# Seven products instead of eight for two more chunks, one of the sums moved to TensorE, and a new order of all steps

## The chip, the core and the metric

The kernel runs on one core of one Trainium2 chip. The metric is device time in microseconds, the median over runs; lower is better. Five engines work side by side, each in the order of its own queue: TensorE (PE, matrix products from on-chip memory into the PSUM banks), VectorE (DVE), ScalarE (ACT), GpSimd (POOL) and SyncE (SP). In this kernel POOL and SP mostly issue transfers (DMAs). An engine waits on semaphores for what another engine or a transfer has to finish first.

## The reference, cut to what matters

```
phi(x) = where(x > 0, x, exp(x) - 1) + 1          # = min(exp(x), max(x, 0) + 1)
kv  = einsum('bhsd,bhse->bhde', phi(k), v)        # per head: 64 x 64
z   = sum over s of phi(k)
x   = (phi(q) @ kv) / (phi(q) . z + 1e-6)         # 8 sequences, 8 heads, 576 x 64 each
a   = x @ w1 ;  b = x @ w2                        # x is 4608 x 512, w1 and w2 are 512 x 1024
out = ((a * b) @ w3) @ w_out                      # 1024 x 1024, 1024 x 512
```

Linear attention on 8 sequences, then a feed-forward part whose two branches are multiplied element by element. w3 @ w_out does not depend on the tokens.

## The kernel before, in words

The 4608 tokens are worked as nine chunks of 512. Chunks 0 to 7 are the first 512 tokens of sequences 0 to 7; chunk 8 collects the remaining 64 of each. All matrix products take bf16 and sum in f32.

At the start w3 @ w_out is folded once into a 1024 x 512 matrix (wf_sb): steps w transpose a block of w3 on TensorE (L143 to L148), steps u multiply it with w_out (L150 to L157), two matmuls of 512 columns a step.

The attention of a sequence b is made of small steps. L, M, N load k, q, v in halves of 512 KB (L97), R loads the last 64 tokens of the eight heads, 64 KB a transfer (L108). x and X take exp on ScalarE (L175), y and Y the max part on VectorE (L181), z and Z their min (L199), v casts v (L212). K sums phi(k) times v over the tokens (L227). T transposes phi(q) by a DMA (L266); for sequences 0 and 1, a does it on TensorE (L271). A multiplies phi(q) by kv for 128 tokens and divides (L288): four matmuls, then three VectorE instructions (L324 to L326); it uses the two "at" PSUM banks, of which there is one pair. D transposes the result by a DMA (L344), for sequences 0 and 1 step P on TensorE (L337).

A gate unit F c.f (L370) makes 128 of the 1024 gate columns of chunk c: eight matmuls of 512 columns (four for a, four for b), a ScalarE copy of a (L367), and a VectorE multiply of that copy with b in PSUM (L368).

Chunks 6, 7 and 8 make their gates differently. The 2 x 2 block product is done with seven products of half-size blocks instead of eight (the Strassen-Winograd scheme). Steps e form four combinations of the blocks of w1 and of w2 once (L386), steps d four combinations of a chunk's x (L398), each one VectorE instruction. A step G c.q.i (L435) is product i of column block q: four matmuls of 256 columns, a pair for each branch (L410). Products 1, 3, 5 and 7 add up in one PSUM bank ("u", one of the two banks that output units use as well, L444), product 2 has a bank of its own ("t"), products 4 and 6 share a third ("t2"); t and t2 are two of the four "mm" banks. The order of a block is fixed by its sums: the bank u after product 1 is copied out by ScalarE (L450); so it is after product 3, and t2 after product 4. VectorE adds such a copy to the bank after product 2, 5 or 6 (L454). A step m c.q.i (L462) multiplies the two halves of such a sum, out of SBUF, into the gate. After product 7 the bank u is multiplied directly: ScalarE copies its a half (L458), VectorE multiplies it with the b half in PSUM (L459). The f32 copies and sums live in a ring of twelve half tiles that takes six slots of the load pool "ld" (L427).

An output unit O c.m (L532) multiplies 128 tokens' gates with wf_sb: eight matmuls of 512 columns and one copy. S, H store results; Q is the last output unit, in two halves with a store each.

The order is written out by hand: the string ORDER (L577) names every step, and each engine's queue gets its instructions in that order. A "+" behind a step chooses the other engine for its copy (VectorE instead of ScalarE) or the other queue for its load (POOL instead of SP). B, C, E are the loads of w1/w2, w_out and w3, always on POOL; they cast f32 to bf16. I are constants. GATES (L613) lets the load M2.1 wait for the weights' load B0.0.

Of the kernel before, what the change touches and what calls it, by code (L numbers as in the profile page):

```python
# [20 lines left out]
def kernel(  # L21
# [403 lines left out]
    ring = []  # L425

    def fsm(name):  # L427
        if not spare.get("ring"):
            spare["ring"] = True
            for n in range(6):  # L430
                t = from_ld(("f", n), [P, 2, 2, HN], F32)
                ring.extend((t[:, 0], t[:, 1]))
        return ring.pop(0)

    def g_unit(c, q, i):  # L435
# [3 lines left out]
        a, m, name, first = ((), ((0, 0, 0), (0, 0, 0), "u", True), ((0, 0, 1), (0, 1, 0), "t", True),  # L439
# [8 lines left out]
        if i in (1, 3, 4):  # L448
            s = st["s", i] = fsm("gs")
            nc.scalar.copy(out=s, in_=t)  # L450
        elif i in (2, 5, 6):
            s = st["c", i] = fsm("gc")
            o = st["s", {2: 1, 5: 4, 6: 3}[i]]
            nc.vector.tensor_tensor(out=s, in0=o, in1=t, op=ALU.add)  # L454
            ring.append(o)
        else:
            s = fsm("ga")
            nc.scalar.copy(out=s[:, 0], in_=t[:, 0])  # L458
            nc.vector.tensor_mul(out=abs_[c][:, q + 4, 0:HN], in0=s[:, 0], in1=t[:, 1])  # L459
            ring.append(s)  # L460

    def g_mul(c, q, i, alt):  # L462
        s = cs_[c, q]["c", i]
        f, r = {2: (q, 0), 5: (q + 4, 1), 6: (q, 1)}[i]
# [125 lines left out]
    A3.0 O1.2 A3.2 L4.1 v4.2+ F2.6 A3.3 F2.3 N4.1 y4.0 F2.1 M4.0 x4.0 A3.1 x4.1 F2.0 M4.1 y4.2 v5.2+  # L590
    x4.2 F2.7 Y4.0 D3.0 F2.4 z4.0 F2.2 X4.1 Y4.1 S1.0 F2.5 v4.1 Z4.1 N4.0 M5.0 X4.0 Z4.0 A3.4 z4.2
    y4.1 O2.3 F3.7 z4.1 M5.1 v4.0 A2.4 Y5.0 F3.6 L5.0 T4.0 M6.1 R6.0+ x5.2 Y5.1 X5.0 F3.1 N5.1 Z5.0
    S1.1 O2.2+ K4 F3.2 M6.0 x6.2 X5.1 A4.2 Z5.1 F3.4 z5.2 F3.5 y5.0 A4.1 F3.0 L5.1 F3.3 N5.0 y5.1
    X6.1 y6.2 O2.1 A4.3 R6.1+ N6.0 S2.1 x5.1 N6.1 v5.0+ T5.0 O2.0 x5.0 v5.1+ A4.0 R7.0+ z5.1 D4.0
    z5.0 X6.0 O3.3 y7.2 O3.2+ K5+ S2.0 L6.0 z6.2 O3.1 A5.2 L6.1 O3.0 A5.1 D1.1 Y6.1 Z6.1 F4.2 A5.0
    Y6.0 F4.5 y6.1 F4.7 v6.0+ x6.1 L7.0 x6.0 M7.0 A5.3 D3.1 x7.0 z6.1 F4.0 v6.1+ v6.2 F4.6 A4.4 Z6.0
    F4.1 S3.0 F4.4 D5.0 A5.4 y6.0 z6.0 F4.3 M7.1 F5.7 x7.2 y7.0 Y7.0 z7.2 L7.1 N7.0 K6+ z7.0 F5.6
    F5.0 y7.1 X7.1 X7.0 Z7.0 F5.5 S3.1 F5.3 Y7.1 T6.0 R7.1+ Z7.1 A6.3 T7.0 F5.1 O4.2 A6.1 x7.1 O4.1
    A6.2 e1.0 e0.0 v7.0 F5.4 A6.0 z7.1 O4.3 e0.1 F5.2 e1.1 v7.2+ O4.0 N7.1 S4.1 e0.2 e0.3 e1.2 D6.0
    d6.0 v7.1 A6.4 e1.3 O5.1 O5.0 G6.1.1 G6.1.2 d6.1 G6.0.1 K7 d6.2 d6.3 G6.0.2 G6.0.3 m6.1.2 G6.0.4  # L600
    m6.0.2 S5.0 A7.3 G6.1.3 G6.0.5 G6.1.4 G6.1.5 m6.0.5 G6.2.4 G6.0.6 G6.0.7 G6.1.7 A7.0 G6.1.6
    G6.2.1 S4.0 G6.3.1 D5.1 G6.2.2 G6.2.3 G6.3.2 G6.3.3 m6.1.6 G6.2.5 G6.3.4 m6.2.2 G6.3.5 G6.2.6
    G6.2.7 A7.4 D7.1 G6.3.7 G6.3.6 O5.2 m6.3.5 A7.2 d8.0 O5.3 d8.2 G8.0.1 G8.0.4 m6.2.6 d8.1 m6.0.6
    d8.3 A7.1 G8.1.1 m6.3.6 G8.0.3 G8.0.2 G8.1.3 m6.2.5 G8.1.4 G8.0.5 G8.1.5 G8.3.4 G8.1.6 m8.0.2
    G8.0.7 G8.1.7 G8.2.4 m6.1.5 D7.0 G8.1.2 m8.0.5 d7.0 G8.2.1 S5.1 G8.3.1 G8.0.6 G8.2.3 m8.0.6
    G8.2.6 G8.3.3 G8.2.5 m6.3.2 G7.0.4 G8.3.5 G7.1.4 m8.1.2 G8.2.7 d7.1 G8.2.2 G8.3.7 d7.2 m8.1.5
    G8.3.6 O6.0 m8.3.5 m8.1.6 d7.3 O6.3 m8.2.5 O6.2+ m8.3.6 m8.2.6 O6.1 G7.0.1 m8.2.2 G8.3.2 G7.1.1
# [122 lines left out]
```

## Time and profile before

| | |
|---|---|
| median of three runs | 250.67 us (249.24 to 251.13) |
| span of the profiled execution | 248.0 us |
| TensorE busy | 230.9 us, 1548 matmuls |
| VectorE busy | 187.4 us, 434 instructions |
| ScalarE busy | 131.9 us, 213 instructions |
| GpSimd busy | 49.4 us, 79 instructions |
| matmuls of the gate units (L362) | 384 of 512 columns |
| matmuls of the seven-product steps (L422) | 336 of 256 columns |
| matmuls of the output units (L536) | 280 of 512 columns |

The profile is of one execution; its span goes from the first to the last instruction, and no total time is given for that execution. The page first gives busy time by engine, then 40 equal slices of the span with the busy share of each engine in tenths. Groups of instructions have a line, an engine, the tiles written and read, a count, the busy time, the mean length in ns, and the idle time before them with what ended it. "The chain" is the work that ended last, followed back step by step. "The waits" list who waited for whom. Matmuls overlap one another, so the time that TensorE needs for one is read from the spacing of starts and not from its length; the same holds, to a lesser degree, for VectorE.

### The profile page before, as it was taken

To read this page: it belongs to the slowest core of one execution; us is meant where nothing else is said; L and a number is where in the kernel's file an instruction comes from. 1 tells how busy PE (TensorE), PEld (TensorE's weight loads), DVE (VectorE), ACT (ScalarE), POOL (GpSimd) and SP (SyncE) were. 2 spreads that over 40 slices of the span, in tenths; PEclk is the share of its full clock that TensorE was granted. 3 is DMA by queue.
4 is the path that set the end of the run, shared out by engine and by line. 5 is a ranking of instruction groups with operands and counts; after the bars stand their busy time and mean duration, and the time that the engine had idled before them with its cause. 6 is when DMAs were issued, how large, how long until landed. Compare 5 with 4: busy or idle time off the path is not lost.

```text
span 248.0 us, 4281 instructions
## 1 busy us (share of the span) xinstructions
PE 230.9 (93%) x1548; PEld 133.6 (54%) x1548; DVE 187.4 (76%) x434; ACT 131.9 (53%) x213; POOL 49.4 (20%) x79
## 2 busy tenths in 40 slices
PE   0699868999999999999999999999999999999994
PEld 0445455654454554345445544545488688578542
DVE  3227769777898847788768799988899999779810
ACT  2206667658756725675563383536466377245321
POOL 8546368665014050500000000000000000000000
PEclk9999988999999999999999999999999999999999
DMA  7999999999999999999999999917750133040144
GB/s 159 193 202 310 295 211 211 194 259 288 287 219 329 236 234 273 217 304 282 288 362 268 284 270 221 295 37 174 169 193 0 22 65 107 3 169 1 44 152 145
DMA packets 64021, 49.43 MB, mean 199 GB/s; under 512 B 32480, under 2 KB 58848, under 8 KB 64000
## 3 DMA queue, kind: packets, MB, share of 16 engines
q1 hardware_dynamic: 52928, 36.31, 58.3%
q0 software_dynamic: 10928, 12.72, 25.2%
q8 instruction: 12, 0.20, 0.3%
q10 hardware_dynamic: 144, 0.13, 0.2%
q14 instruction: 9, 0.07, 0.1%
HBM read 38.80 MB, written 9.44 MB: 194 GB/s over the span
## 4 chain that ended last, share of the span: by engine, by line
PE 67%; DMA 21%; ACT 3%; DVE 3%; SPq 2%; issue 2%; POOL 0%; ACTq 0%; DVEq 0%; POOLq 0%
PE o_ps L536 21%; PE a_ps L362 12%; PE b_ps L362 12%; DMA q<-in_q_dram 10%; PE gu L422 9%; DMA w3b<-in_moe_w_dram 7%; PE gt L422 6%; DMA k<-in_k_dram 4%; PE nd L310 3%; PE kvp L245 2%; SPq L104 1%; ACT e L179 1%; PE o_ps L561 1%; PE kvp L249 1%; DVE qj L209 1%
## 5 line engine op out<-in xcount | busy, mean ns | idle before, releaser
L536 PE MATMUL o_ps<-wf_sb,ab 128*128 128x512 bf16 x280 | 64.2, 379 | 0.0
L362 PEld LDWEIGHTS <-w_sb 128*128 128x128 bf16 x384 | 36.5, 98 | 40.6 <-issue 0.8
L362 PE MATMUL a_ps<-xt,w_sb 128*128 128x512 bf16 x192 | 50.3, 379 | 0.5 <-ACT a_sb L367 0.5
L362 PE MATMUL b_ps<-xt,w_sb 128*128 128x512 bf16 x192 | 50.3, 379 | 0.0
L536 PEld LDWEIGHTS <-ab 128*128 128x128 bf16 x280 | 26.8, 98 | 29.3
L368 DVE TENSOR_TENSOR ab<-a_sb,b_ps 128x512 bf16<-128x512 f32 x48 | 32.5, 683 | 11.5 <-PE b_ps L362 5.9
L538 ACT COPY o_sb<-o_ps 128x512 f32<-128x512 f32 x30 | 17.4, 585 | 42.8 <-PE o_ps L536 28.8
L367 ACT COPY a_sb<-a_ps 128x512 f32<-128x512 f32 x48 | 27.7, 585 | 22.2 <-PE a_ps L362 21.8
L326 DVE TENSOR_TENSOR xn<-nd,r 128x512 bf16<-128x512 f32 x30 | 20.7, 691 | 1.0
L422 PEld LDWEIGHTS <-spare 128*128 128x128 bf16 x192 | 18.7, 98 | 2.2
L179 ACT ACTIVATE e<-q 128x1024 bf16<-128x1024 f32 x16 | 16.8, 1057 | 5.7 <-DMA q<-in_q_dram 5.0
L310 PE MATMUL nd<-kv,qt 128*128 128x130 bf16 (+1 forms) x160 | 16.6, 228 | 2.9 <-ACT kv L254 1.8
L179 ACT ACTIVATE e<-k 128x1024 bf16<-128x1024 f32 x16 | 16.8, 1056 | 3.2 <-DMA k<-in_k_dram 3.1
L310 PEld LDWEIGHTS <-qt 128*128 128x128 bf16 (+1 forms) x160 | 11.8, 103 | 12.2 <-issue 3.5
L454 DVE TENSOR_TENSOR spare<-spare,gt 128x512 f32<-128x512 f32 x24 | 16.1, 680 | 1.8 <-PE gt L422 0.9
L154 PE MATMUL wf_ps<-wt_sb,w3t 128*128 128x512 bf16 x64 | 16.5, 403 | 0.6 <-DMA wt_sb<-in_moe_w_out_dram 0.6
L450 ACT COPY spare<-gu 128x512 f32<-128x512 f32 x24 | 13.6, 587 | 3.9 <-PE gu L422 3.7
L422 PEld LDWEIGHTS <-w_sb 128*128 128x128 bf16 x144 | 14.0, 98 | 2.7 <-issue 0.3
L465 DVE TENSOR_TENSOR ab<-spare 128x256 bf16<-128x256 f32 x36 | 14.1, 417 | 0.1
L114 POOL DMA_DIRECT2D qk32r<-in_q_dram x14 | 9.0, 644 | 23.3 <-ACT a_sb L367 10.7
L209 DVE TENSOR_TENSOR qj<-e,y 128x512 bf16<-128x512 bf16 x32 | 12.1, 418 | 2.0 <-ACT e L179 1.8
L422 PE MATMUL gu<-spare 128*128 128x256 bf16 x96 | 13.4, 272 | 0.0
(87 smaller groups left out, 294.0 us busy)
## 6 DMA issues: line engine op xcount, KB each, us to landing
out_dram<-o_sb SPq DMA_DIRECT2D x15, 512.0 KB, 3.9
q<-in_q_dram SPq DMA_DIRECT2D x13, 512.0 KB, 8.1
k<-in_k_dram SPq DMA_DIRECT2D x12, 512.0 KB, 7.0
v<-in_v_dram SPq DMA_DIRECT2D x12, 512.0 KB, 9.0
w3b<-in_moe_w_dram POOLq DMA_DIRECT2D x8, 256.0 KB, 10.0
k<-in_k_dram POOLq DMA_DIRECT2D x4, 512.0 KB, 9.1
w_sb<-in_moe_w_dram POOLq DMA_DIRECT2D x8, 256.0 KB, 7.5
q<-in_q_dram POOLq DMA_DIRECT2D x3, 512.0 KB, 12.6
```

The lines of the kernel that those rows point to most:

```text
L154: nc.tensor.matmul(wfs[i], w3ts[i][:, kc, :], wo_sb[:, kc, :], start=(kc == 0), stop=(kc == FC - 1))
L179: nc.scalar.activation(out=e, in_=x, func=AF.Exp)
L209: nc.vector.tensor_tensor(out=p[0][:, 2 * g + c].rearrange("p j u d -> p u j d"), in0=e[:, c], in1=y[:, c], op=ALU.min)
L310: nc.tensor.matmul(nds[g][rows, i * 2 * E1:(i + 1) * 2 * E1], w, kvs[b % 2][:, i, g].rearrange("p u e -> p (u e)"), start=True, stop=True)
L326: nc.vector.tensor_tensor(out=dst.rearrange("p (g h) e -> p g h e", g=2), in0=v4[:, :, :, 0:D], in1=r[rows].unsqueeze(3).to_broadcast([n, ...
L362: nc.tensor.matmul(ps, w[:, kc, f * P:(f + 1) * P], xt_of(c)[:, :, kc, :], start=(kc == 0), stop=(kc == KC - 1))
L367: nc.scalar.copy(out=a_sb, in_=a_ps)
L368: nc.vector.tensor_mul(out=abs_[c][:, f, :], in0=a_sb, in1=b_ps)
L422: nc.tensor.matmul(t[:, w], l, r, start=(first and w == 0 and k == 0), stop=(k == 1), skip_group_check=True)
L454: nc.vector.tensor_tensor(out=s, in0=o, in1=t, op=ALU.add)
L536: nc.tensor.matmul(o_ps, ab[:, f, m * P:(m + 1) * P], wf_sb[:, f, :], start=(f == 0), stop=(f == FC - 1))
L538: copy_of(alt)(out=rows_of(c, m // 2)[:, m % 2], in_=o_ps)
```

## The change

Three things are done together.

1. Chunks 4 and 5 also make their gates with the seven products: F4.* and F5.* go, d4.*, d5.*, G4.*, G5.*, m4.*, m5.* come. Chunks 0 to 3 keep the gate units.
2. In all five such chunks, product 2 no longer has a VectorE add. After product 1 ScalarE copies bank u into an "mm" bank instead of into SBUF, and the four matmuls of product 2 accumulate onto that bank. Its result is then treated like that of product 7: ScalarE copies the a half, VectorE multiplies it with the b half in PSUM; these copies use the small tiles of the gate units ("f", four of them). The steps m c.q.2 vanish. The ring has eight half tiles, in four slots of the load pool. The combinations of w1 are kept in the tile that held w_out, so that only those of w2 take slots of the load pool.
3. ORDER is new from the first step to the last. It begins with loads of k and q beside those of w3 and w_out, so that the attention of sequence 0 (K0) comes ahead of the products u. The loads L2 to L5, L6.1, M2 to M6, N2 to N5 and N6.0 (28 loads) go from SP to POOL, as do R0.0 and R0.1; R6.1, R7.0 and R7.1 go from POOL to SP. Some copies change engine (K0 to VectorE; K1, K5, K6 to ScalarE; some of O, P, a, u, v, w). The order of the chunks (0 to 6, then 8, then 7) stays.

```diff
@@ ws_make
+        if w == 0:
+            s[i] = wt_sb[:, i].rearrange("p a n -> p (a n)").rearrange("p (k n) -> p k n", k=2)
+        else:
+            s[i] = from_ld(("w", w, i // 2), [P, 2, 2, NQ * P], BF16)[:, i % 2]
@@ fsm
-            for n in range(6):
+            for n in range(NR):                       # NR = 4
@@ g_unit
-        ... ((0, 0, 1), (0, 1, 0), "t", True),
+        ... ((0, 0, 1), (0, 1, 0), "t", False),
-        if i in (1, 3, 4):
+        if i == 1:
+            st["t"] = mm_ps.tile([P, 2, HN], F32, tag="mm", name="gt")
+            nc.scalar.copy(out=st["t"], in_=t)
+        elif i in (3, 4):
             s = st["s", i] = fsm("gs")
             nc.scalar.copy(out=s, in_=t)
-        elif i in (2, 5, 6):
+        elif i in (5, 6):
             s = st["c", i] = fsm("gc")
-            o = st["s", {2: 1, 5: 4, 6: 3}[i]]
+            o = st["s", {5: 4, 6: 3}[i]]
             nc.vector.tensor_tensor(out=s, in0=o, in1=t, op=ALU.add)
             ring.append(o)
         else:
-            s = fsm("ga")
-            nc.scalar.copy(out=s[:, 0], in_=t[:, 0])
-            nc.vector.tensor_mul(out=abs_[c][:, q + 4, 0:HN], in0=s[:, 0], in1=t[:, 1])
-            ring.append(s)
+            s = sm.tile([P, NCH], F32, tag="f", name="a_sb", bufs=4)[:, 0:HN]
+            nc.scalar.copy(out=s, in_=t[:, 0])
+            nc.vector.tensor_mul(out=abs_[c][:, q if i == 2 else q + 4, 0:HN], in0=s, in1=t[:, 1])
```

The new order, its start and the stretch in which chunks 4 and 5 are gated:

```
E3 L0.0+ x0.0 R0.0+ C1 L0.1+ R0.1+ y0.1 I0 y0.0 E0 M0.1+ E5 N0.0+ N0.1 C0 z0.0 E7 x0.1 C3 z0.1
C2 E1 M0.0 Y0.0 I1+ M1.1+ E6 Y0.1 X0.0 E2 M1.0+ Z0.0 R1.1+ X0.1 L1.0+ x0.2 v0.2 L1.1+ Z0.1 B3.1
y0.2 z0.2 w0+ B3.0 R1.0+ N1.1 N1.0 w3 w5+ K0+ a0.0+ B2.0 B2.1 E4 a0.1 u5.0 u5.1 u0.0 w7+ a0.2
...
O3.3 O3.2 S3.1 v5.1+ x6.2 N5.0+ z5.0 v5.0 O2.3 Y5.0 M6.0+ Z5.0 z5.2 T5.0 x6.1 z5.1 A4.4 N7.1
d4.0 z6.2 X6.0 L6.0 O3.0 d4.1 O3.1 G4.0.1 K5 G4.1.1 S3.0 d4.2 Y6.1 Z6.1 Y6.0 Z6.0 G4.0.3 y6.1
d4.3 G4.0.4 N6.1 A5.3 G4.0.2 G4.1.3 G4.0.5 G4.1.4 A5.2 G4.1.5 G4.0.7 G4.0.6 D3.1 N6.0+ G4.1.2
A5.1 G4.3.4 G4.1.7 v7.1 O2.2 y6.0 A5.0 m4.0.6 z6.1 G4.3.1 G4.1.6 R6.1 G4.2.1 G4.3.3 m4.0.5
G4.3.2 G4.2.3 G4.3.5 m4.1.6 D5.0 N7.0 G4.2.4 G4.2.5 G4.2.2 G4.3.7 v6.2 G4.3.6 G4.2.7 v6.1 d5.0
d5.1 m4.2.5 x6.0 G4.2.6 O4.1 z6.0 m4.1.5 G5.0.1 G5.0.4 G5.1.1 G5.0.3 m4.3.6 d5.2 T6.0 v6.0+ d5.3
...
G5.3.4 A6.2 m5.0.6 G5.3.5 G5.3.2 Y7.0 v7.0 L7.1 O4.0 M7.1 y7.2 G5.3.6 G5.3.7 x7.2 m5.3.6 A5.4
z7.2 R7.1 D6.0 m5.2.6 d6.0 X7.1 S4.0 O5.0 m5.1.6 x7.1 O4.3 d6.1 v7.2 d6.3 O4.2 d6.2 Y7.1 Z7.1
...
K7 G6.2.3 m5.1.5 m5.3.5 m5.2.5 D5.1 O5.3 G6.2.5 G6.2.2 G6.3.1 G6.2.6 G6.2.7 A7.4 G6.3.3 D7.1
...
m8.2.5 O8.1 S8.0 O8.2+ H8.2 O8.3 H8.3 O7.2+ H7.2 Q7.3
```

More of the change, by code (lines that the diff above doesn't have):

```diff
@@ L425 @@
     ring = []
+    NR = 4
     def fsm(name):
@@ L438, in g_unit @@
         st = cs_.setdefault((c, q), {})
-        a, m, name, first = ((), ((0, 0, 0), (0, 0, 0), "u", True), ((0, 0, 1), (0, 1, 0), "t", True),
+        a, m, name, first = ((), ((0, 0, 0), (0, 0, 0), "u", True), ((0, 0, 1), (0, 1, 0), "t", False),
                              ((1, 1), (1, 1), "u", False), ((1, 0), (1, 0), "t2", True),
@@ L604 @@
[L604 to L607, printed above, removed]
-    m8.3.2 G7.0.3 S6.0 G7.0.6 G7.1.3 G7.0.5 G7.0.2 G7.1.5 G7.3.4 m7.1.5 G7.0.7 G7.2.4 m7.0.6 G7.1.7
-    G7.1.6 m7.0.2 G7.2.1 G7.2.2 G7.3.1 S6.1 m7.2.2 G7.2.3 G7.2.6 G7.3.3 G7.2.5 G7.3.6 G7.3.5 G7.2.7
```

57 lines of the change are left out of this document (27 added, 30 removed).

## The prediction

> **What bounds the kernel now.** I read the page's engine totals and slices first, then the busy time by stretch, the waits, and last the chain in order of time.
>
> ```profile
> span 248.0 us, 4281 instructions
> PE 230.9 (93%) x1548; PEld 133.6 (54%) x1548; DVE 187.4 (76%) x434; ACT 131.9 (53%) x213; POOL 49.4 (20%) x79
> PE   0699868999999999999999999999999999999994
> DVE  3227769777898847788768799988899999779810
> PEclk9999988999999999999999999999999999999999
> ```
>
> The reader is to see a TensorE row that is full from the seventh slice to the last but one, and a VectorE row that reaches 9 only after the twenty-third. A busy PE need not be a PE at its rate, so the next view is the chain, where the pieces are spaced by what the array really took:
>
> ```profile
> 61.23 0.86 PE a_ps L362 x4
> 62.09 0.86 PE b_ps L362 x4
> 184.68 0.87 PE gu L422 x8
> 185.55 0.44 PE gt L422 x4
> 230.68 12.09 PE o_ps L536 x56
> ```
>
> Here 56 matmuls of 512 columns take 12.09 us, 0.216 each, and a matmul of 256 columns takes 0.87/8 = 0.109. The gate units (L362) run at the same 0.86/4 = 0.215. So in these stretches TensorE runs without holes, and work taken from it is worth its full length, as long as nothing else becomes late. What else could be late is seen by stretch (columns: stretch, length, then busy time and instructions of PE, PEld, DVE, ACT, POOL):
>
> ```profile
> 98.00:131.00 33.00, 31.80 (x175) 15.14 (x174) 26.16 (x57) 20.80 (x32) 3.94 (x6) 1.00 1.10 295
> 131.00:180.00 49.00, 49.00 (x284) 24.29 (x282) 43.30 (x99) 23.66 (x37) 0.00 (x0) 1.00 0.90 211
> 180.00:212.00 32.00, 32.00 (x289) 26.48 (x287) 30.67 (x72) 19.86 (x39) 0.00 (x0) 1.00 0.26 75
> ```
>
> From 180 to 212 us, where chunks 6 and 8 are gated by seven products, VectorE is busy 30.67 of 32 us (96%), and TensorE still does not stop: both engines are at their limit there. From 131 to 180, with chunks 4 and 5 gated plainly, VectorE has 5.7 us free. That is the room the change spends. What TensorE waited for after the start is little:
>
> ```profile
> PE nd L310 <- DVE xn L326: 0.8, 2, 0.5
> PE a_ps L362 <- ACT a_sb L367: 0.5, 1, 0.5
> PE nd L310 <- DVE xnr L326: 0.2, 1, 0.2
> ```
>
> These add to 1.5 us.
>
> **The change part by part.**
>
> *TensorE, chunks 4 and 5.* Removed: 16 gate units (F4.*, F5.*) of 8 matmuls, 128 x 0.216 = 27.6 us. Added: 56 products (G4.*, G5.*) of 4 matmuls of 256 columns, 224 x 0.109 = 24.4 us. Net -3.2 us. Every other TensorE step is there as often as before; products of chunks 6 to 8 are the same.
>
> *VectorE.* Durations overlap with the next instruction's, so I take the spacing of starts where the engine has no idle time (rows of the timeline; the two without an operation name are pieces of the chain):
>
> ```profile
> 195.85 0.42 DVE L459 TENSOR_TENSOR ab<-spare,gu 128x256 bf16<-128x256 f32 x1
> 196.19 0.68 DVE L454 TENSOR_TENSOR spare<-spare,gt 128x512 f32<-128x512 f32 x1
> 196.78 0.42 DVE L465 TENSOR_TENSOR ab<-spare 128x256 bf16<-128x256 f32 x1
> 197.12 0.16 DVE L324 TENSOR_SCALAR r<-nd 128x8 f32<-128x8 f32 x1
> 197.31 0.20 DVE L325 RECIPROCAL r<-r 128x8 f32<-128x8 f32 x1
> 197.55 0.69 DVE L326 TENSOR_TENSOR xn<-nd,r 128x512 bf16<-128x512 f32 x1
> 34.44 0.76 DVE qj L209 x2
> 35.20 0.60 DVE y L184
> 46.30 1.28 DVE L368 TENSOR_TENSOR ab<-a_sb,b_ps 128x512 bf16<-128x512 f32 x2 [0.63 <-ACT a_sb L367]
> ```
>
> An add of 512 columns costs 0.59, a multiply of 256 columns 0.34, an attention block (A) 0.19 + 0.24 + 0.6 = 1.04, a max step (y) 0.60, a min step (z, a pair whose second half overlaps) 0.67, a plain gate multiply 1.28 - 0.68 = 0.60. A difference of x (d) I put at 0.34, the multiply's price, since it covers 512 bf16 columns as one L209 does (0.76/2 at most).
> Chunks 4 and 5: minus 16 x 0.60; plus, for both, 8 differences, 16 adds (products 5, 6) and 32 multiplies (products 2, 5, 6, 7): 16 x 0.59 + 40 x 0.34 = 23.0. Net +13.4. Chunks 6 to 8: product 2 loses its add, and its multiply stays, 12 x 0.59 = -7.1. Together +6.3 us: VectorE goes from 187.4 to about 194 of 248.
>
> *ScalarE.* Chunks 4, 5: minus 16 copies of 512 columns, plus 24 (products 1, 3, 4), plus 16 of 256 (products 2, 7); chunks 6 to 8: plus 12 of 256.
>
> ```profile
> L450 ACT COPY spare<-gu 128x512 f32<-128x512 f32 x24 | 13.6, 587 | 3.9 <-PE gu L422 3.7
> L458 ACT COPY spare<-gu 128x256 f32<-128x256 f32 x12 | 4.5, 373 | 4.9 <-PE gu L422 4.2 <-DVE ab L459 0.5
> ```
>
> That is 8 x 0.587 + 28 x 0.373 = +15.1, to 147 of 248: hidden behind TensorE while ScalarE has two fifths of its time free. No row shows a ScalarE copy that writes PSUM. The bounds are the 256-column copy (0.37) and twice the 512-column one (1.17); I take 0.587, the same size from the same bank. At the upper end the 20 such copies add 12 us to an engine that still has 89 free. New is that product 2 waits for this copy. In the new order the closest pair (G4.3.1, G4.3.2) has three products between, 1.3 us of TensorE against 0.59 of copying; it is hidden unless ScalarE is 0.7 us behind. What stands behind a late product 2 is every matmul, since TensorE's queue is in order.
>
> *The stretch where both engines are full.* In the new order I sum the steps from O2.3 up to O5.3 (the rest of chunk 2's output, chunks 4 and 5 gated, the attention of sequences 5 to 7, the first half of chunk 6). Two more prices from the chain:
>
> ```profile
> 109.92 0.41 PE nd L310 x4
> 133.84 0.45 PE kvp L245 x8
> 134.29 0.11 PE kvp L249
> 134.40 0.45 PE kvp L245 x8
> ```
>
> TensorE: 10 output units, 73 products, 11 attention blocks, 3 kv sums, 10 x 1.73 + 73 x 0.437 + 11 x 0.35 (0.41 less the overlap at its end) + 3 x 1.1 = 56 us. VectorE: 20 adds 11.8, 39 multiplies 13.3, 12 differences 4.1, 11 attention blocks 11.4, 9 max 5.4, 10 min 6.7, and some 2 us of tails and a v copy: 54.7 us. So for 56 us VectorE must be as full as it was in 180 to 212 for 32, and its load comes early: behind O3.1 stand d4.2, four steps of sequence 6 (Y, Z) and d4.3 while TensorE goes on with products. TensorE cannot run that far ahead: an attention block takes the only "at" bank pair, freed by the block before on VectorE; an output unit (O4.1, O5.0, O5.3) needs all its multiplies. Summed from O2.3 with the same prices, TensorE is at 22.0, 40.5 and 56.3 us when it comes to these three, and VectorE at 21.5, 39.6 and 54.6 when their last multiply is through, if it never waits. It does wait: a multiply at a block's end comes about 0.4 us behind its product (the ScalarE copy), and at 96% VectorE reaches 22.4, 41.3 and 56.9. That makes holds of 0.4 to 0.8 us at each, some 2 us in all with the blocks A5.2 and A5.0. Bounds: none, as in 180 to 212; and 6 us, if VectorE is no fuller than 88% (43.30/49, its share in 131 to 180): 54.7/0.88 = 62. I take +2.0, since the row with products is the nearer one.
>
> *The start.* Order and queues of the loads change; the bytes don't. Two rows of TensorE's timeline, two transfers on the chain (issue, time to landing), one of VectorE's and three of POOL's, and the landing times of the eight loads of w1 and w2 (L125):
>
> ```profile
> 5.91 1.04 PE L147 MATMUL w3p<-ident,w3b 128*128 128x128 bf16 x8 [5.91 <-DMA w3b<-in_moe_w_dram]
> 41.62 1.02 PE L362 MATMUL a_ps<-xt,w_sb 128*128 128x512 bf16 x4
> 22.08 0.68 DVE L184 TENSOR_SCALAR y<-k 128x1024 bf16<-128x1024 f32 x1
> 8.60 11.74 DMA w3b<-in_moe_w_dram
> 20.62 12.62 DMA q<-in_q_dram
> 20.62 0.75 POOL L104 DMA_DIRECT2D q<-in_q_dram  x1 [0.53 <-DMA w3b<-in_moe_w_dram]
> 21.98 1.08 POOL L104 DMA_DIRECT2D q<-in_q_dram  x1 [0.61 <-DMA k<-in_k_dram]
> 43.01 1.60 POOL L125 DMA_DIRECT2D w_sb<-in_moe_w_dram  x2 [1.08 <-DMA k<-in_k_dram]
> DMA to landing us min/median/max: 5.7/7.5/8.5
> ```
>
> The load issued at 8.60 landed at 20.34, the eighth after it at 33.24: one per 1.6 us. Before, TensorE begins at 5.9 us with w4. Now the first transposes (w0) need E0, behind E3, L0.0, C1, L0.1 and six small tails on POOL's queue: 5.9 + 4 x 1.6 + 6 x 0.4 (an estimate, a quarter of a whole load) = about 15 us, and the first kv sum (K0) four loads later, 21. The wf products that filled 10 to 30 us now follow K0. But the gate units of chunk 0 need w1 and w2, and these end where they ended: the last pair was issued from 43.01 and landed within 8.5 us, about 52 us, with the same bytes ahead of it. Between 25 and 52 us TensorE has the postponed wf products to do while it waits. Against 41.62 I get the first gate unit at 39 to 41, with 2.7 us of work (u4.*, w4, a1.0) moved behind it. So 0, with bounds of -1.5 (the loads alone decide) and +2 (one stop more, as the clock then drops: its slice row has two 8s where TensorE's row falls to 6 and 8, 31 to 43 us).
>
> *Loads on another queue.* 28 loads of sequences 2 to 6 go from SP, where they stood between transposes and stores that wait, to POOL; 8 tail DMAs go the other way. R6.1, R7.* and the last M, L, N stay on SP behind T and D. TensorE's idle time after the start lies mostly where SP carried these loads: from 98 to 131 us it is busy 31.80 of 33 us, 1.2 of the 1.5 us of waits. I take -0.7, half of these, with bounds of -1.5 and, by the third rival, +2.5. Two issues on POOL show the risk: 1.08 us against 0.75, and VectorE's row shows the one max step that ran meanwhile. The Trainium skill, "SBUF — State Buffer" (section "SBUF: two separate sides", the "DVE blocks DMA" trap), says that POOL cannot write a DMA's descriptors while VectorE runs an op that takes both SBUF ports; the 0.33 us here agrees in sign, and by it the 28 loads would lose about 9 us of a POOL queue that is idle 80% of the time; so the sum stays as it is, unless the loads have no lead, which is the third rival.
>
> *At nothing:* the reuse of the output weights' tile for w1's combinations (they wait for the last wf product, which stands 70 steps ahead; without that distance one 0.60 VectorE step would stand still); four ring tiles in place of six (product 2 no longer takes them; if the eight halves run out, a ScalarE copy waits for a multiply, 0.34); copies that change between VectorE and ScalarE (about even); the tail, which still ends O8.3, O7.2, Q7.3.
>
> Sum against the profiled span: 248.0 - 3.2 + 2.0 + 0 - 0.7 = 246.1, so -1.9. The three runs lie 1.2 to 3.1 above that span; against their median, 250.67 - 1.9 = 248.8 us.
>
> **The rivals.**
> 1. *VectorE paces chunks 4 to 6 (slower).* Place: O2.3 to O5.3. For it: the sums 54.7 and 56; 40 multiplies and 20 bank hand-offs that each wait for another engine. Against it: 96% in 180 to 212. The gain of 3.9 is gone when the holds reach 3.9 us, VectorE at 91% (54.7/59.9), and from there on it is slower; at 84% they are 9 us, less the 2 us that may be made up after O5.3: 250.67 - 3.9 + 7 = 253.8.
> 2. *The lag is absorbed (faster).* The 2 us of holds vanish, since multiplies and max steps can be late without anyone waiting: 246.8; with the start at its lower bound 245.3. For it: 180 to 212 again, and chunks 6 to 8 are lighter by 0.59 a column block.
> 3. *Loads late.* POOL's queue runs at 1.6 us a load with others waiting in line; each of the five sequences brings one stop like the longest of TensorE's waits, 0.5: 248.8 + 0.7 + 2.5 = 252.0. Against it: POOL has nothing else to do after 60 us, and no stores stand between its loads. The rule of the Trainium skill's SBUF page works to this side; it adds 0.01 to this rival's chance.
> 4. *A worse start.* w0 at 15 us and the clock low again: 250.8.
>
> **How the numbers follow.** My forecast (holds of 1 to 3 us, start within 1) has 0.46 and its own range of 247.3 to 250.5; rival 1 has 0.19, rival 2 0.22, rival 3 0.06, rival 4 0.07. That the products don't save TensorE time I exclude by the chain. About 1% (2.5 us) is what a measurement of this kernel can tell from no change. Faster by it means under 248.2: all of rival 2 and a third of the forecast, 0.37. Slower means over 253.2: most of rival 1 and a little of rival 3, 0.16. Within: 0.47. The range reaches from rival 2 with two thirds of its start gain, 245.8, to rival 1, 253.8.
>
> **What would show it.** Right: L362 falls to 256 matmuls and L422 rises to 560 at 0.109; VectorE 93 to 97% busy for some 50 us before the last third, with TensorE's waits there "PE nd <- DVE xn" and "PE o_ps <- DVE ab", 1 to 3 us; first gate unit at 39 to 41 us. Wrong: waits of products on the ScalarE copy into PSUM over 0.5 us in total; q or k loads that end TensorE's waits after 60 us; VectorE under 90% in that stretch while TensorE has holes.

## The result, and the profile after

The kernel after takes 265.31 us (median of 4 runs, 264.0 to 266.22) against 250.77 us of the kernel before in the same session: 1.0586 times as long, 95% interval 1.0532 to 1.0640. The forecast was 248.8 us. The profiled execution has a span of 262.2 us (before: 248.0). Times and ratios here are those of undisturbed executions; the profiles of e2, e7 and e9 are of longer, disturbed ones and serve for their waits and landing times, not for their spans.

The page, the same rows as before (span, engines, slices of TensorE, VectorE and the clock):

```profile
span 262.2 us, 4532 instructions
PE 229.6 (88%) x1644; PEld 143.3 (55%) x1644; DVE 196.7 (75%) x461; ACT 144.5 (55%) x250; POOL 69.9 (27%) x105
PE   0028999999999969889479999999999999999994
DVE  0096889687989628798536999999999789879541
PEclk9999999999999997999959999999999999999999
```

TensorE's row, full from the eighth slice in the kernel before, now has a 6 and a 4, and the clock has a 7 and a 5 in the same slices or right behind them. The stretches behind the two holes (columns as in the prediction: stretch, length, busy time and instructions of PE, PEld, DVE, ACT, POOL; then granted clock, DMA share, GB/s):

```profile
99.00:103.00 4.00, 4.00 (x15) 1.74 (x14) 3.72 (x10) 0.62 (x2) 1.07 (x2) 0.57 1.00 307
133.00:137.00 4.00, 4.00 (x13) 1.51 (x12) 1.59 (x5) 0.59 (x1) 0.00 (x0) 0.52 0.07 26
```

A hole costs its length here, and then about 4 us at a granted clock of 0.57 or 0.52, at which half a gate unit takes 1.71 us in place of 0.86. The waits of TensorE (total us, times, longest):

```profile
PE w3p L147 <- DMA w3b<-in_moe_w_dram: 15.5, 1, 15.5
PE nd L310 <- DMA qt<-qj: 5.3, 1, 5.3
PE a_ps L362 <- ACT a_sb L367: 3.1, 2, 2.5
...
PE a_ps L362 <- DMA xt<-xn: 0.7, 1, 0.7
```

The second is a wait of an attention block for phi(q), transposed by a DMA (T4.0). The waits shown of the kernel before have none like it. The chain around the two holes (start, length, piece):

```profile
88.57 8.32 DMA out_dram<-o_sb
...
98.60 1.23 PE a_ps L362 x4
...
103.44 9.14 DMA xt<-xn
112.58 20.05 DMA qt<-qj
...
132.68 0.61 PE nd L310 x4
```

A store of 512 KB, 8.32 us under way, holds back a ScalarE copy and with it a gate unit; that this store is late because of the moved loads is not shown (in the kernel before, stores took up to 11.4 us). Then two transposed transfers follow each other on SP's queue, and the second, T4.0, takes 20.05 us from its issue to its landing. By stretch:

```profile
88.00:104.00 16.00, 13.49 (x73) 6.51 (x71) 8.32 (x19) 4.14 (x10) 7.85 (x13) 0.89 1.03 234
104.00:133.00 29.00, 21.96 (x119) 10.15 (x118) 21.04 (x40) 14.14 (x23) 9.93 (x14) 0.95 1.10 272
137.00:205.00 68.00, 67.40 (x531) 47.06 (x529) 62.22 (x154) 50.97 (x94) 1.15 (x1) 1.00 0.74 180
205.00:255.00 50.00, 50.00 (x378) 35.55 (x377) 38.78 (x89) 25.51 (x53) 0.00 (x0) 1.00 0.27 74
```

From 88 to 133 us TensorE stands 9.6 us and runs at a clock of 0.89 and 0.95; in the stretch of the products, 137 to 205, it stands 0.6 us, with VectorE at 91%. To put this in one sum I count TensorE's work by the spacings of the prediction (0.216 for 512 columns, 0.109 for 256, and so on); what is left of the time is idle time, slow clock included:

| us | work | idle to 90 us | idle 90 to 137 | idle 137 to the end | last matmul |
|---|---|---|---|---|---|
| before | 220.9 | 19.9 | 2.1 | 1.4 | 244.3 |
| after | 217.8 | 23.2 | 14.5 | 2.95 | 258.5 |
| change | -3.1 | +3.3 | +12.4 | +1.5 | +14.2 |

So the work, counted this way, fell as forecast, the products' stretch cost less than forecast, and 15.7 us came from the first half. Of the 14.5 us from 90 to 137 the waits that the trace names from 42 to 137 us are 9.7, and the slow clock in the two stretches above is about 3.6 (an estimate: 4.00 x 0.43 + 4.00 x 0.48). T4.0's share is its wait of 5.3 us and the second of the slow stretches.

### The profile page after: what moved, and what is told of

Read it like the earlier page. It is cut to its first block, busy times and chain, and to the rows that moved or that the text cites. A ratio compares the mean times of both kernels' runs of the same rounds, so it can differ in the third digit from the quotient of the medians.

```text
span 262.2 us, 4532 instructions
## 1 busy us (share of the span) xinstructions
PE 229.6 (88%) x1644; PEld 143.3 (55%) x1644; DVE 196.7 (75%) x461; ACT 144.5 (55%) x250; POOL 69.9 (27%) x105
## 4 chain that ended last, share of the span: by engine, by line
PE 66%; DMA 21%; DVE 5%; ACT 4%; issue 2%; POOL 1%; ACTq 0%; DVEq 0%; SPq 0%; POOLq 0%
PE o_ps L542 17%; PE gu L425 13%; PE gt L425 9%; DMA qt<-qj 8%; PE a_ps L362 7%; PE b_ps L362 7%; DMA out_dram<-o_sb 5%; DMA xt<-xn 3%; PE nd L310 3%; PE wf_ps L154 3%; DMA k<-in_k_dram 3%; DMA q<-in_q_dram 2%; PE kvp L245 1%; PE w3p L147 1%; ACT o_sb L544 1%
## 5 line engine op out<-in xcount | busy, mean ns | idle before, releaser
L362 PEld LDWEIGHTS <-w_sb 128*128 128x128 bf16 x256 | 25.0, 101 | 33.7 <-issue 7.9
L362 PE MATMUL a_ps<-xt,w_sb 128*128 128x512 bf16 x128 | 35.4, 393 | 4.0 <-ACT a_sb L367 3.1
L362 PE MATMUL b_ps<-xt,w_sb 128*128 128x512 bf16 x128 | 35.6, 395 | 0.4 <-ACT a_sb L367 0.4
L368 DVE TENSOR_TENSOR ab<-a_sb,b_ps 128x512 bf16<-128x512 f32 x32 | 21.9, 684 | 15.8 <-PE b_ps L362 7.9
L544 ACT COPY o_sb<-o_ps 128x512 f32<-128x512 f32 x27 | 15.7, 586 | 32.2 <-PE o_ps L542 22.4
L367 ACT COPY a_sb<-a_ps 128x512 f32<-128x512 f32 x32 | 18.6, 587 | 26.6 <-PE a_ps L362 23.5
L425 PEld LDWEIGHTS <-w_sb 128*128 128x128 bf16 x240 | 23.2, 98 | 5.5 <-issue 1.4
L147 PE MATMUL w3p<-ident,w3b 128*128 128x128 bf16 x64 | 5.9, 253 | 18.5 <-DMA w3b<-in_moe_w_dram 15.5
L184 DVE TENSOR_SCALAR y<-k 128x1024 bf16<-128x1024 f32 x16 | 12.0, 756 | 13.4 <-DMA k<-in_k_dram 13.2
L310 PEld LDWEIGHTS <-qt 128*128 128x128 bf16 (+1 forms) x160 | 11.6, 101 | 13.4 <-DMA qt<-qj 5.8
L425 PEld LDWEIGHTS <-spare 128*128 128x128 bf16 x160 | 15.6, 98 | 1.8
L425 PEld LDWEIGHTS <-wt_sb 128*128 128x128 bf16 x160 | 15.0, 98 | 2.9 <-DVE spare L410 0.6
L471 DVE TENSOR_TENSOR ab<-spare 128x256 bf16<-128x256 f32 x40 | 15.7, 420 | 0.2
L147 PEld LDWEIGHTS <-w3b 128*128 128x128 bf16 x64 | 5.1, 115 | 19.6 <-DMA w3b<-in_moe_w_dram 17.1
L104 POOL DMA_DIRECT2D v<-in_v_dram x9 | 7.2, 799 | 31.6 <-DVE y L184 31.6
```

Source lines behind the costliest of these rows:

```text
L147: nc.tensor.transpose(tp[:, kc, :], raw["w3", i // 4][:, i % 4, kc * P:(kc + 1) * P], ident)
L310: nc.tensor.matmul(nds[g][rows, i * 2 * E1:(i + 1) * 2 * E1], w, kvs[b % 2][:, i, g].rearrange("p u e -> p (u e)"), start=True, stop=True)
L362: nc.tensor.matmul(ps, w[:, kc, f * P:(f + 1) * P], xt_of(c)[:, :, kc, :], start=(kc == 0), stop=(kc == KC - 1))
L367: nc.scalar.copy(out=a_sb, in_=a_ps)
L368: nc.vector.tensor_mul(out=abs_[c][:, f, :], in0=a_sb, in1=b_ps)
L425: nc.tensor.matmul(t[:, w], l, r, start=(first and w == 0 and k == 0), stop=(k == 1), skip_group_check=True)
```

## The experiments

Theory 1 after the result: the 28 loads on GpSimd's queue make SP's transposes late. Its rival: the new order does it, and the queue is innocent.

**The queue.** e2 is the kernel before with nothing but the 28 loads moved.

```diff
 ORDER of the kernel before
-... P1.1 M2.1 M3.1 ... L2.1 ... N2.1 ... L4.0 ... N6.0 ...
+... P1.1 M2.1+ M3.1+ ... L2.1+ ... N2.1+ ... L4.0+ ... N6.0+ ...
```

> The kernel before with one thing done: the same 28 loads go to POOL, nothing else moves. Theory 1: the transposes of sequences 3 to 6 land later than 10 us after their issue and TensorE waits for them, 255 to 263 us. Theory 2: the queue of the loads does not matter, 249.5 to 252 us.

Measured: 273.65 to 277.24 us, 1.0977 (1.0886 to 1.1068). That alone is more than the whole change. TensorE's two largest waits, two pieces of e2's chain, and the landing times of the six T transposes (min, median, max), first e2, then the kernel before, then the kernel after:

```profile
PE nd L310 <- DMA qt<-qj: 14.8, 1, 14.8
PE kvp L249 <- DVE vr L221: 12.1, 1, 12.1
...
68.88 15.71 DMA v32r<-in_v_dram
...
94.84 22.71 DMA qt<-qj
```

```profile
DMA to landing us min/median/max: 4.6/8.3/22.7
```

```profile
DMA to landing us min/median/max: 4.6/7.1/9.8
```

```profile
DMA to landing us min/median/max: 4.6/5.5/20.1
```

The first wait is for a transposed phi(q), as in the change. The second is not: it ends with a 64 KB load of the last rows of v (R). Most of these loads were on GpSimd's queue in the kernel before too, where they landed in 5.7 to 8.1 us; in e2 this one stands behind moved loads and takes 15.71. So the move makes late what stays on SP's queue and also what stood on GpSimd's.

How the transposes starve is seen in the queue part of the page (packets, MB, share of the 16 engines), of the kernel before and of e2:

```profile
q1 hardware_dynamic: 52928, 36.31, 58.3%
q0 software_dynamic: 10928, 12.72, 25.2%
```

```profile
q0 software_dynamic: 14960, 27.40, 42.0%
q1 hardware_dynamic: 38144, 21.63, 34.4%
```

The 28 loads are 14.7 MB. On SP's queue (q1) they were 14,784 packets, 528 a load, of which 512 carry 1 KB each and 16 four bytes; on GpSimd's (q0) they are 4,032, 144 a load, 128 of 4 KB and 16 of four bytes. In the kernel after, between 120 and 130 us, the trace's packet records show 176 to 190 packets in every 2 us on q0 and, within 2, as many on q1: 655 KB a stretch against 45 to 49 KB. In these 10 us the queues take turns, and a packet of the transpose has 256 bytes. When q0 ran dry, at 130 us, q1 moved 314 KB in 2 us and T4.0 landed. The Trainium skill, "DMA: Bandwidth & Descriptors" (section "Queues, rings and completion order"), says that an engine takes turns between its queues at the granularity of a packet; the counts of this stretch agree. They are not equal everywhere: in e2 from 72 to 80 us GpSimd's queue gets 17 to 51 packets in 2 us and SP's 212 to 441, and what sets the shares there is not shown. In the kernel before there was little to take turns with: these loads and the transposes stood in line on one queue, and GpSimd's had only the 64 KB loads by then.

e4 takes the load from T4.0's way: the loads behind R5.0 wait until T4.0 has landed.

```diff
-    GATES = "R6.0<T3.0 M2.1<B0.0"
+    GATES = "R6.0<T3.0 M2.1<B0.0 R5.0<T4.0"
```

> The changed kernel with one more gate: POOL's load R5.0, and with it every load behind it on POOL, waits until the transpose T4.0 has landed. Theory 1: T4.0 lands 5 to 8 us after its issue instead of 20, the stop of 5.5 us at 127 us and the slow clock behind it go, 257 to 260 us, if the loads held back are not missed later. Theory 2: T4.0 was late because its data were, 264 to 267 us.

Measured: 262.18 us, 1.0458 (1.0381 to 1.0535). Landing times of T and the largest wait after the start:

```profile
DMA to landing us min/median/max: 4.6/5.0/7.9
```

```profile
PE kvp L245 <- DVE vt L215: 5.4, 1, 5.4
```

T4.0 now lands 4.6 us after its issue, so the loads had made it late; but the loads held back are missed themselves, 5.4 us in place of 5.3. The mechanism of theory 1 held, its time did not (two runs).

e1 undoes the move in the kernel after.

```diff
 ORDER of the kernel after
-... L2.0+ ... N2.1+ ... M3.0+ ... N6.0+ ...
+... L2.0 ... N2.1 ... M3.0 ... N6.0 ...
```

> The changed kernel with one thing undone: the 28 loads of sequences 2 to 6 go to SP again, in the places where the new order names them. Theory 1, the transposing DMAs starve beside loads on POOL's queue (both queues share the 16 DMA engines, and the transposes' small packets get one turn for each large packet): the 12.5 us that TensorE lost between 95 and 137 us go, 253 us, give or take 2; T4.0 lands within 10 us of its issue. Theory 2, the new order itself is late there (VectorE, banks, D1.1 too early): 263 to 267 us, with the same holes.

Measured: 292.12 us, 1.1656 (1.1595 to 1.1717): neither theory. TensorE's waits:

```profile
PE a_ps L362 <- ACT a_sb L367: 16.4, 2, 10.8
...
PE kvp L245 <- ACT vt L215: 9.3, 2, 8.4
```

One of the waits of SP's queue in the same run:

```profile
SPq L269 <- DVE qj L209: 34.0, 3, 12.3
```

Transposes land within 7.2 us again, but three of them stand at the head of SP's queue for 34.0 us in all until their input is there, and loads and stores stand behind them. So in the new order the loads need the second queue, and the second queue starves the transposes: taking back the queue alone makes the kernel slower still. How much of the 12.4 us from 90 to 137 is the queue's and how much the new order's is therefore not separated by these runs.

e6 was to halve the loads' packets by issuing each load of sequences 4 to 6 as two transfers of 256 KB.

> The kernel after, but each load of k, q, v of sequences 4 to 6 on GpSimd's queue is issued as two transfers of two heads (256 KB) in place of one of four, so that each of their packets carries half as much. Theory 1 (the queues take turns packet by packet, and a 256-byte transpose packet waits for a whole load packet): T4.0 lands 9 to 14 us after its issue in place of 20, D1.1 7 to 9 in place of 12, and the time is 258 to 262 us. Theory 2 (the transposes are late because the memory traffic as a whole is full): T4.0 lands 18 to 21 us after its issue as before, 264 to 267 us.

Measured: 261.87 us, 1.0429 (1.0347 to 1.0511), T4.0 after 20.8 us. The queue row of the kernel after, and of e6:

```profile
q0 software_dynamic: 14896, 27.27, 43.1%
```

```profile
q0 software_dynamic: 15152, 27.27, 44.1%
```

The 16 loads brought 256 packets more, 16 each and not 128, and the trace's records show that these are packets of four bytes, while the data still went in packets of 4 KB: the packets did not halve, and the run misses its point. Why it is 3.4 us faster than the change (two runs), with T4.0 as late, stays open. What smaller packets would do wasn't tried.

**The start.** e7 is the kernel after with the old order up to F0.7; e5 is the same with the 28 loads on SP.

```diff
 ORDER of the kernel after (e7)
-E3 L0.0+ x0.0 R0.0+ C1 ... F0.7 ...
+(the kernel before, from its first step to F0.7), then the steps left, in the new order
```

> The kernel after, but with the order of the kernel before up to F0.7 (the first gate unit's neighbourhood), and from there the new order with its loads on GpSimd's queue. Theory 1 (the start's 3.3 us are a term of their own, kept to the end): 261 to 262.5 us. Theory 2 (the time from 90 to 137 us is set by the transfers, which don't begin earlier, so a better start is waited away there): 264 to 266 us.

> The kernel of the first run here (loads on SP), and the order begins with the steps of the kernel before up to its first gate unit F0.7; the rest follows in the new order. It asks for the start alone: the changed kernel's TensorE is 2.9 us further behind its work at 42 us than the kernel before. If the order of the first steps does this, it is 2 to 3.5 us faster than the first run here, near 250 us under theory 1; if the loads of w1 and w2 set the pace anyway, it is equal to it within 1 us. Theory 2: 260 to 264 us.

Measured: e7 1.0297 (1.0177 to 1.0418; 256.79 and 260.35 us) against the change's 1.0586. e5 290.18 us, 1.1595 (1.1522 to 1.1668), where e1 had 1.1656; TensorE's idle time at 42 us is 18.1 us in e5 and 22.2 in e1, and of these 4.1 us 2 are left in the time. The start is a cost of its own, some 3 to 4 us at 42 us; that e7 won back more, 4 to 10 us by its interval, stays unexplained, for T4.0 is as late there (21.6 us).

**The products, with the new order behind the old front.** e8 keeps the order and the queues of the kernel before up to K4 (117 us), then goes on in the new order; e9 cuts later, at O2.0.

> The order and queues of the kernel before up to K4 (about 110 us), then the new order for the rest, with the weight combinations spread over the next gate units; chunks 4 and 5 by seven products, product 2 accumulated in PSUM. Only four of the 28 loads stay on GpSimd's queue. Theory 1 (the seven products are worth TensorE -3.2 and VectorE holds +1.5 wherever they stand, and all of the loss lies in the front): 248 to 250 us, 1.0 to 2.5 us under the kernel before. Rival 3 (the stretch was only cheap because TensorE came to it 14 us late and the other engines were ahead; without that lag VectorE at 91% and more paces it): holds of 4 to 8 us, 251 to 256 us.

> As the last one, but the order of the kernel before up to O2.0 (about 125 us), with the weight combinations right behind one another and two of the loads left on GpSimd's queue. Theory 1: 248 to 250 us, again 1.0 to 2.5 us under the kernel before. Rival 3: 251 to 256 us, with TensorE's holds at A and O steps behind VectorE between 130 and 190 us.

Measured: e8 252.18 to 255.67 us, 1.0124 (1.0078 to 1.0171); e9 254.36 and 256.65 us, 1.0176 (1.0080 to 1.0271), in whose profile a T transpose holds TensorE for 6.1 us. e8 lies in the range of rival 3, and e9's two runs lie about its upper end. But an order put together from two has waits at its seam, so three kernels take e8 apart without moving the seam: e14 with chunks 4 and 5 by plain gate units, e11 with chunk 4 alone plain, e12 with product 2 the old way.

```diff
 ORDER of e8 (e11: chunk 4 alone; e14: both)
-... d4.0 ... G4.0.1 ... G4.1.1 ... d4.3 ... m4.0.5 ...
+... F4.0 ... F4.4 ... F4.1 ...
 g_unit (e12)
-        if i == 1:
-            st["t"] = mm_ps.tile([P, 2, HN], F32, tag="mm", name="gt")
-            nc.scalar.copy(out=st["t"], in_=t)
-        elif i in (3, 4):
+        if i in (1, 3, 4):
             s = st["s", i] = fsm("gs")
...
-        elif i in (5, 6):
+        elif i in (2, 5, 6):
```

> The kernel of the old front up to K4 (254.4 us), with chunk 4 gated by eight plain gate units again, spread over the places of its products; chunk 5 stays with seven products. TensorE +1.6 us, VectorE about -6.7 us of which none elsewhere. Rival 1 (VectorE paces): the holds fall by more than 1.6 us, 251 to 253.5 us. Theory 2 (the holds do not depend on the products): 255.5 to 256.5 us.

> The kernel of the old front up to K4 (254.4 us), with chunks 4 and 5 both gated by plain gate units, at the places of their products; so the seven products for these two chunks are undone alone, in the new order. TensorE +3.2 us, VectorE -13.4 us. Rival 1 (VectorE paces): the holds after 130 us all but vanish, 251 to 253.5 us. Theory 2 (the holds come from the order): 257 to 258 us.

> The kernel of the old front up to K4 (254.4 us), with product 2 the old way in all five chunks: a PSUM bank of its own, a VectorE add, the multiply as a step right behind, a ring of twelve half tiles in six load slots. TensorE as it was; VectorE +20 x 0.59 = 11.8 us, 4.7 of them in chunks 4 and 5. Rival 1 (VectorE paces): 4 to 9 us more, 258 to 264 us. Theory 2 (VectorE has room): 253.5 to 256 us. The two load slots that it takes from late loads can add up to 2 us in either case.

Measured: none of the two chunks by products 1.0188 (1.0143 to 1.0233), chunk 5 alone 1.0143 (1.0094 to 1.0192), both 1.0124, both with product 2 the old way 1.0527 (1.0451 to 1.0602). e11 and e12 lie in the ranges of rival 1, e14 in neither of its two. The intervals of the first three overlap, so the traces have to tell them apart. The last unit that TensorE does in all four before the first product or gate unit of chunk 4 is O3.0. Its row and TensorE's last row, in e8, e14, e11 and e12:

```profile
138.19 3.61 PE L542 MATMUL o_ps<-wf_sb,ab 128*128 128x512 bf16 x16 [0.33 <-ACT o_sb L544]
...
247.15 1.91 PE L567 MATMUL o_ps<-wf_sb,ab 128*128 128x256 bf16 x16
```

```profile
137.92 3.61 PE L542 MATMUL o_ps<-wf_sb,ab 128*128 128x512 bf16 x15 [0.33 <-ACT o_sb L544]
...
247.98 1.91 PE L567 MATMUL o_ps<-wf_sb,ab 128*128 128x256 bf16 x16
```

```profile
137.45 3.61 PE L542 MATMUL o_ps<-wf_sb,ab 128*128 128x512 bf16 x15 [0.33 <-ACT o_sb L544]
...
245.76 1.91 PE L567 MATMUL o_ps<-wf_sb,ab 128*128 128x256 bf16 x16
```

```profile
136.34 3.61 PE L539 MATMUL o_ps<-wf_sb,ab 128*128 128x512 bf16 x15 [0.33 <-ACT o_sb L541]
...
254.70 1.91 PE L564 MATMUL o_ps<-wf_sb,ab 128*128 128x256 bf16 x16
```

From O3.0 to the end e8 takes 249.06 - 138.19 = 110.9 us, e14 112.0, e11 110.2 and e12 120.3. So in one and the same order the products of both chunks bring 1.1 us of TensorE's 3.2, and the holds that come with them take 2.1. By the same rows chunk 5's products bring 1.8 us, all of their 1.6, and chunk 4's cost 0.7, so the holds are chunk 4's; these are differences of single executions. Product 2 on PSUM is what makes the products bearable: with its 20 adds on VectorE (11.8 us) e12 is 9.4 us longer from the same mark. TensorE's largest waits there, from 136 us on:

```profile
PE nd L310 <- DVE xn L326: 2.6, 3, 2.1
PE gu L425 <- DVE spare L458: 2.2, 5, 0.6
PE o_ps L539 <- DVE ab L463: 1.9, 4, 0.7
```

With two smaller ones 7.9 us of waits are behind VectorE, so that VectorE paces e12, rival 1's mechanism, is shown (e12 also takes two more slots of the load pool, which is not separated). That it paces e8 is not: there one wait of 1.4 us is behind VectorE, and e14, with 13.4 us less for VectorE and 3.2 more for TensorE, is 1.1 us longer.

e10 was to relieve VectorE: combinations and differences of x on GpSimd (a "+" behind e and d4, d5).

> The kernel of the old front up to K4 (254.4 us), with the 8 combinations of the weights and the 8 differences of x for chunks 4 and 5 made by GpSimd, which is idle there, in place of VectorE: 8 x 0.6 + 8 x 0.34 = 7.5 us less for VectorE between about 110 and 190 us, nothing else changed. Rival 1 of the prediction (VectorE paces this stretch): TensorE's holds behind VectorE shrink by 2 us or more, 250.5 to 252.5 us. Theory 2 (the holds are waits between single steps of an order put together from two, and not a matter of VectorE's load): 254 to 257 us.

Measured: 266.69 us, 1.0687 (1.0640 to 1.0734). Rows of GpSimd, then VectorE's of the same time (start, length):

```profile
112.76 2.12 POOL L399 TENSOR_TENSOR spare<-w_sb,spare 128x1024 bf16<-128x1024 bf16 x1 [6.08 <-ACT a_sb L367]
114.84 2.31 POOL L399 TENSOR_TENSOR spare<-w_sb 128x1024 bf16<-128x1024 bf16 x1
117.11 2.29 POOL L399 TENSOR_TENSOR wt_sb<-w_sb,wt_sb 128x1024 bf16<-128x1024 bf16 x1
```

```profile
113.57 6.45 DVE L209 TENSOR_TENSOR qj<-e,y 128x512 bf16<-128x512 bf16 x4
120.05 0.17 DVE L324 TENSOR_SCALAR r<-nd 64x8 f32<-64x8 f32 x1
```

Four min steps, two of which take 0.76 elsewhere, take 6.45 us and end 0.6 us after GpSimd's last sum. The relief blocked the engine that it was to relieve, so this run tells nothing of rival 1.

**The products in the old order.** The last group keeps the old order and the old queues as long as possible. e17 is the kernel before up to O5.0 and then the new order, chunks 4 and 5 plain: what is left of the change is product 2 on PSUM and the last third. e15 and e16 replace the gate units of both chunks, or of chunk 5, by products in an arrangement of my own (two column blocks at a time). e18 cuts at Z6.1, just ahead of chunk 4's gates, and goes on as the new order does, e19 keeps chunk 4 plain, and e20 is e18 with the seam mended.

```diff
 ORDER of e18, and of e20
-... O3.0 A5.1 D1.1 Y6.1 Z6.1 S3.1 x6.1 A4.4 N7.1 d4.0 d4.1 G4.0.1 G4.1.1 S3.0 d4.2 Y6.0 Z6.0 G4.0.3 ...
+... O3.0 A5.1 d4.0 d4.1 D1.1 S3.1 N7.1 G4.0.1 G4.1.1 S3.0 d4.2 d4.3 G4.0.3 G4.0.4 Y6.1 G4.0.2 A5.3 ...
```

> As the last ones, but chunks 4 and 5 both keep plain gate units: all that is left of the change is product 2 in PSUM in chunks 6 to 8 (VectorE -7.1 us there) and the new order from chunk 6 on. TensorE's work as before, 1.4 us of waits after 137 us to be won at most. Theory 1: 249.5 to 250.7 us. Rival (the new order of the last third costs by itself): 251 to 253 us.

> The order and the queues of the kernel before up to O5.0 (about 178 us), with only the gate units of chunks 4 and 5 replaced by seven products at their places, written by me two column blocks at a time, the weight combinations earlier; product 2 accumulated in PSUM in all five chunks; from chunk 6 on the new order. No load changes queue. Theory 1 (the terms of the prediction for TensorE, -3.2, and VectorE's holds, +1.3 to +2.0, are right by themselves): 248.5 to 250 us. Rival 1 (VectorE paces whatever the order): 251.5 to 255 us.

> As the last one, but chunk 4 keeps its plain gate units: half of the products, TensorE -1.6 us, VectorE +3.2 in the stretch. Theory 1: 249 to 250 us. Rival 1: 250.5 to 252 us.

> The order and queues of the kernel before up to Z6.1, just ahead of chunk 4's gates (about 137 us), with the weight combinations spread over chunks 2 and 3 from about 85 us on; from there the new order with chunks 4 and 5 by seven products. Theory 1 (the products gain by themselves once their steps are interleaved as finely as in the new order): TensorE -3.2, holds +1.3 to +2.0, 248.5 to 250 us. Rival 1 (VectorE paces, whatever the order): 251.5 to 255 us.

> As the last one, but chunk 4 keeps its plain gate units in the old order, and the new order begins with chunk 5's products (about 150 us): half of the products, TensorE -1.6 us. Theory 1: 249 to 250 us. Rival 1: 250.5 to 253 us.

> As the kernel cut at Z6.1 (256.25 us), with the seam between the two orders mended: the four differences d4 and the first products stand ahead of the max and min steps of sequence 6, and A4.4, whose output tile waits for the transfer D1.1, stands behind 13 products instead of ahead of d4. That kernel was level with the kernel before up to 137 us and lost 7.9 us there by 150 us, 4.1 of them in one hole. Theory 1 (the products gain by themselves): the 7.9 us shrink to 1 or 2, 249 to 251 us. Rival 1 (VectorE paces and the hole only moves): 252 to 256 us.

Measured: e17 250.02 us, 0.9997 (0.9968 to 1.0026): product 2 on PSUM and the new last third neither cost nor gain, as forecast. e15 268.8 us (1.0758) and e16 265.09 us (1.0608), with TensorE waiting for VectorE at the ends of my column blocks (7.4 us in three waits for the multiply that frees a bank in e15): they price that arrangement. e18 254.44 to 256.57 us, 1.0196 (1.0144 to 1.0247); e19 250.56 to 254.01 us, 1.0057 (1.0022 to 1.0092); e20 254.64 us, 1.0173 (1.0117 to 1.0229). Up to 137 us e18 is level with the kernel before (21.8 us of idle time against 22.0), and loses 7.9 us by 150. VectorE's row there, and TensorE's:

```profile
144.12 0.68 DVE L326 TENSOR_TENSOR xnr<-nd,r 64x512 bf16<-64x512 f32 x1 [2.61 <-DMA xtr<-xnr]
```

```profile
145.65 0.61 PE L425 MATMUL gu<-spare,wt_sb 128*128 128x256 bf16 x2 [3.94 <-DVE spare L410]
```

VectorE stood for a tile that the transfer D1.1 still read, with the differences of x behind it. e20 puts A4.4 later and the differences first, and the hole moves: 2.2 us for an output copy whose tile a store still reads, 1.9 us for a VectorE sum, 6.1 us lost from 137 to 150. In e19 the one large wait is 3.0 us, an output unit for the last multiply of chunk 4. By their times e19 and e20 lie in the ranges of rival 1, but the largest holds in these traces are at single steps of the seams. No order that was tried here beats the kernel before.

## Why the prediction was wrong

- **TensorE's work, -3.2: right.** L362 has 256 matmuls, L425 560; counted at the old spacings, TensorE does 3.1 us less.
- **"Loads on another queue: I take -0.7": the step that failed.** The stretch where these loads are on their way measured +12.4 in the change, and the move alone cost +9.8% (about 24 us) on the old order. The bounds, -1.5 and +2.5, asked whether the 28 loads would come late on the new queue. In the change no wait of TensorE after the start ends with a moved load. What failed is that the step priced the loads that moved and not the transfers that they would share with: the T transposes that stayed on SP and had to take turns with packets 16 times as large (T4.0 landed after 20.05 us; 5.3 us of wait, and half the clock behind it), and, in e2, the 64 KB loads behind them on GpSimd's queue (12.1 us of wait). What the queue cost within the new order stays open, since e1, which takes it back, is slower still. The prediction's rival 3 (252.0 us) had the right part of the change and the wrong victim; its price of 0.5 us a sequence was far too small. The sign to look for was named as "q or k loads that end TensorE's waits"; what ended the longest was the transpose of q. Against that rival stood that GpSimd "has nothing else to do after 60 us"; but it issued loads of the last rows of v until 105 us, in the kernel before:

```profile
L114 POOL DMA_DIRECT2D v32r<-in_v_dram x14: 617/617/679, 36.8 to 105.3; - x14
```

- **"The start: 0, with bounds of -1.5 and +2": wrong in size.** Its landmarks were right, w0 at 15.5 us and K0 at 21.2. But the first gate unit came at 41.91 us and not at 39 to 41, with the 2.7 us of postponed work still to do: +3.0, and +3.3 by 90 us. e7 shows it to be a cost by itself.
- **VectorE's holds, +2.0: the size was near, the mechanism is not shown.** The change has +1.5 there, but its trace names no wait of TensorE for VectorE after 137 us, and TensorE came to this stretch some 14 us late, so that the others could be ahead: the nearness is partly luck. In e8 against e14, without that delay, the holds are 2.1. VectorE was 91% busy there, not the 93 to 97% forecast, and 196.7 us in all, not about 194; the trace of the change has no wait "nd <- DVE xn" there. Rival 1 priced at 253.8 us did not decide the change; e12 shows where it would have: 4.7 us more on VectorE in that stretch, and 7.1 later.
- **The first reading of the page was off by a little.** TensorE's row of the kernel before is full from the eighth slice (its seventh digit is an 8), and VectorE's has a 9 in the seventh and the twelfth slice. No term of the sum hangs on it.
- **ScalarE's copy into PSUM, 0.587 hidden: right.** Group rows of the copy into PSUM and of one into the load pool (count, busy, mean ns):

```profile
L454 ACT COPY gt<-gu 128x512 f32<-128x512 f32 x20 | 11.6, 582 | 1.9 <-PE gu L425 1.3 <-DVE xn L326 0.3
L457 ACT COPY spare<-gu 128x512 f32<-128x512 f32 x20 | 11.8, 591 | 4.0 <-PE gu L425 3.3 <-DVE ab L466 0.4
```

No product waits for it among TensorE's waits.

What stays open: whether the 1.1 us of the products, or the 1.8 of chunk 5 alone, can be had beside a front as good as the old one. e17 says that nothing else of the last third costs, the traces of e8, e11 and e14 that the products gain a little in a given order, and e18 to e20 that each seam tried took more than that.

## What to carry to other kernels

When transfers move to another queue, price first what stays behind: a queue is not only a place to wait, it is also a share of the DMA engines, and a transfer of small packets that stood in line can get one small packet per large one once it has company (T4.0 here). Then price the transfers that were on the other queue already and now stand behind the newcomers (the 64 KB loads in e2). An order and its queues are one thing; undoing one part of such a change (e1: +16.6%) prices neither. A product or a sum is worth what a pair of kernels with the same order shows, and not what a stretch looks like that another stretch has made late.

## What the runs showed of the hardware

- A 512 KB load of 1 KB rows went out as 512 packets of 1 KB from SP and as 128 of 4 KB from GpSimd, each with 16 of four bytes; issued as two transfers on GpSimd (e6) it still had packets of 4 KB, and 16 more of four bytes.
- Beside GpSimd's queue a transposed transfer took 20.05 us, 22.7 in e2; in the kernel before, in line with the same loads, the six took 4.6 to 9.8 us.
- A bf16 sum of 1024 columns takes GpSimd 2.1 to 2.3 us against 0.60 by VectorE's spacing, and VectorE's bf16 steps with two operands stand still meanwhile (e10: four in 6.45 us). The Trainium skill, "SBUF — State Buffer" (section "Who interferes with whom"), says that a VectorE instruction with two SBUF inputs contends with a GpSimd instruction that reads SBUF; the rows agree.
- After TensorE had stood for 5.3 us, the granted clock was 0.52 for the next 4 us, and half a gate unit took 1.71 us in place of 0.86 (the kernel after).
